# Output weights' preparation released earlier, and the first operand sums of a seven-product stage kept in other buffers

## The chip, the cores and the metric

One Trainium2 chip, one core of it. The metric is the device time of one execution in microseconds (us). The shown time before is the median of three runs.

## The reference

Sliding-window attention over 8 batches x 8 heads x 576 positions x 64 dimensions (window 128, a linear bias by distance and head), then a gated feed-forward layer over the 4608 tokens (512 in, 1536 hidden, 512 out), all in float32:

```python
x = attention(q, k, v).transpose(0, 2, 1, 3).reshape(4608, 512)
gate = 1.0 / (1.0 + exp(-(x @ w_gate)))
val = x @ w_val
return (gate * val) @ w_out
```

## The kernel before, in words

**Four kinds of work.** (1) Attention, 32 units (a batch and a pair of heads each). Its result goes to DRAM as `xs`, one piece per batch. (2) The *plain pass* (`ffn`, L646): for the first 3072 tokens, in six tiles of 512, four of the twelve hidden chunks are computed in the ordinary way. Each float32 operand is split into a high and a low part, and three matmuls (high*high, high*low, low*high) stand for one. (3) The *seven-product stage* (`ffn2` with `chunk` and `product`, L780): gate and value are computed together by a seven-product (Strassen-Winograd) scheme on 2x2 blocks. A token group (`GROUPS`: three of 2 x 512 tokens, then two of 2 x 384) is loaded from `xs` into `later_xr`, and eleven preparations follow: four block sums (`add`, L743) and seven splits into `xc0` to `xc6` (`hilo`, `parts`, L201 and L210), used in the order 0, 3, 4, 1, 5, 2, 6. Then each hidden chunk takes seven products of six matmuls, 42 in all, into three PSUM banks (`bx`, `by`, `bz`), with sums and gating on DVE and ACT (L787, L791, L795, and L201 for copies out of PSUM). The hidden rows go to DRAM (`hid`). The order of groups: the two of 384 first (groups 3 and 4, seven chunks each, then five more each), then the three of 512 (eight chunks each). (4) The *output stage* (`last`, L910) multiplies `hid` by the output weights, by the same scheme.

**Weights.** `prepare2` loads a chunk of gate and value weights (`wraw`, decoded at L337, L338, L341), forms four differences (L209 on POOL or L210 on DVE) and splits all seven blocks into a slot `w2s0` to `w2s6`. Slots 0 to 2 lie in a pool that is there from the start; slots 3 to 6 are in a pool that opens when the attention pool closes (`close`, key `"w2pool"`). `prepare_o(n)` does the same for the output weights, in six sets: load two raw chunks, decode into `wbits` and `tt`, four differences, split into `wg` and `wtmp`, store to DRAM as `stash_o`; `fetch_o(n)` later brings a set into slot n. Set n may not start before `OUT0 + OSTEP * n` on the planner's clock (470 + 36 n), and it has the lowest priority of all.

**What sets the order.** The kernel first builds a graph of operations with keys that they read and write, and a list scheduler (`Graph.order`) with a cost for each operation then fixes one order for every engine and for the DMA queue on SP. On the chip each engine, and SP, works through its list in that order. At equal start the operation with the lower `want` goes first: the plain pass has -1.0e6, the first seven-product group -1.0e6 + 0.4, later weights 0.5 to 0.9 above that, attention 0 to some 200, matmuls of the two stages 1.0e6, and `prepare_o` 2.0e6. A `follow(keys)` is an empty operation that writes all its keys: who uses one of them afterwards waits for all earlier users of any.

**Shared places.** `xc0` to `xc6` lie in the buffers `ar0` to `ar6`. Before that, the plain pass keeps its split tokens in `ar0` and `ar1` and its weights in `ar2` to `ar5` (one chunk each, used in the order 2, 3, 4, 5), and attention has the k and q of every third unit in `ar6`. `later_xr` has the buffer `xr`, in which the plain pass loads its tokens and attention has pieces too (`qr2`, `kept`, `spread2`, `xt0`). The scratch for sums, `low`, lies in `h2` with attention's `kr2`. The follow before `ffn2` makes both `xr` and `low` wait for `"w2pool"`. `wtmp0` and `wtmp1`, the large part of a `prepare_o` set, lie in `h3` and `h4`. In the last group of 512 (`ends`), a chunk's hidden rows rotate through four buffers `later_hs0` to `later_hs3` and not two; numbers 2 and 3 lie in `h3` and `h4` as well, so the third and fourth chunk of that group wait for the last set's stores out of `wtmp`.

**Banks.** Attention has PSUM banks 2 to 5 for scores and 6 and 7 for the rest; the plain pass has 0 and 1. The later stages take the eight in turn: 0, 1, 2, ... (`bank`).

Of the kernel before, what the change touches and what calls it, by code (L numbers as in the profile page):

```python
# [8 lines left out]
F32 = mybir.dt.float32  # L9
I32 = mybir.dt.int32  # L10
F32R = mybir.dt.float32r
# [4 lines left out]
P = 128  # L16
B, H, S, D = 8, 8, 576, 64
NPAIR = H // 2
TOK = 2 * S
NBLK = TOK // P  # L20
DM, DFF = 512, 1536
NT = B * S
KC = DM // P
NFC = DFF // P
NB = 512
# [14 lines left out]
KEEP2 = 3  # L40
NPB, NST, NPT, NBOTH = 8, 9, 3, 2
P0, PSTEP = 120.0, 56.0
OUT0, OSTEP = 470.0, 36.0
TRI = 3
VDELAY = 1
VHEAD = 11
# [124 lines left out]
def dve_cost(n, psum=False, two=False):  # L171
    return 0.07 + n * (0.00104 if psum or two else 0.00053)
# [7 lines left out]
def attention_gated_ffn(ctx: ExitStack, tc: tile.TileContext, qd, kd, vd, wg, wv, wo, out):  # L180
    nc = tc.nc
    ctx.enter_context(tc.manual_schedule())
    g = Graph()
# [3 lines left out]
    moe = ctx.enter_context(tc.tile_pool(name="moe", bufs=1))  # L187
    ps_m = ctx.enter_context(tc.tile_pool(name="ps_m", bufs=1, space=PSUM))
    att_ctx = ExitStack()
    att = att_ctx.enter_context(tc.tile_pool(name="att", bufs=1))  # L190
# [3 lines left out]
    def T(pool, name, shape, dtype, tag=None):  # L194
        if name not in made:
            made[name] = pool.tile(shape, dtype, tag=tag or name, name=name)
        return made[name]
# [35 lines left out]
    def keep(tag, *shape):  # L233
        n, (t, a) = 1, spare.get(tag) or (moe.tile([P, ROOM[tag]], F32, tag=tag, name=f"early_{tag}"), 0)
        for x in shape:
            n *= x
        spare[tag] = t, a + n
        names = " ".join("abc"[:len(shape)])
        return t[:, a:a + n].rearrange(f"p ({names}) -> p {names}", **dict(zip("abc", shape)))
# [4 lines left out]
    f = -8.0 * 2.0 ** -1  # L244
# [52 lines left out]
    class First:  # L297
        name, fcs = "w1", list(range(FC1))
# [7 lines left out]
    class Later:  # L306
        name = "w2"
# [6 lines left out]
    def piece_keys(a):  # L314
        keys = [(x, c) for x in ("xhi", "xlo") for c in range(KC)]
        keys += [("w1", kind, p, i) for i in range(FC1) for kind in "gv" for p in range(2)]
        return keys[a * PIECE:(a + 1) * PIECE]

    raws, mms, banks = [0], [0], [2]

    def bank():
        mms[0] += 1
        return (mms[0] - 1) % banks[0]

# [17 lines left out]
    def parts(hi, lo, val, n, reads, k0, k1, want, slack=0.0):  # L344
        copy(hi, val, n, reads, [k0], want, slack=slack)
        minus(lo, val, lambda: as32(hi()), n, [*reads, k0], [k1], want)
# [13 lines left out]
    class Unit:  # L360
# [12 lines left out]
        def rel(self, i):  # L373
# [4 lines left out]

    slots = {("kr", 2): keep("h2", TOK), ("qr", 2): keep("xr", (NBLK + 1) // 2, P),
             ("kr", 0): keep("ar6", TOK), ("qr", 0): keep("ar6", (NBLK + 1) // 2, P)}  # L380
    kept = [keep("h2", TRI, P), keep("xr", TRI, P)]
    spread2 = [keep("xr", TRI, P), keep("h2", TRI, P)]
    xt0 = keep("xr", S)

    def slot(x, u, shape):
        return slots[x, u.l] if (x, u.l) in slots else T(att, f"{x}{u.l}", [P, *shape], F32)
# [222 lines left out]
    FIRST = -1.0e6  # L609
# [66 lines left out]


    def combo(k, part_, n2):
        return T(moe, f"xc{k}", [P, 2, 2, NB], F32R, tag=f"ar{k}")[:, part_, :, 0:n2]

    def prepare2(w, i, fc, want, release=0.0):
        s = bitn[0] % 2
# [44 lines left out]
    def ffn2(t, w, todo, F, ends=False):  # L727
        made = t in held
        held[:] = [t]
        t0, N2 = GROUPS[t]  # L730
        xr = lambda: xrow()
# [4 lines left out]
        m = 2 * N2  # L736
# [3 lines left out]

        def add(o, a, b, op, reads, writes):
            way = ("POOL", 0.1 + m * 0.00223, True, lambda: nc.gpsimd.tensor_tensor(o(), a(), b(), op=op))
            g.add("DVE", dve_cost(m, two=True), lambda: nc.vector.tensor_tensor(o(), a(), b(), op=op), reads + ["w2pool"], writes, F,  # L743
                  port=True, ways=[way])

        if not made:
            for h in range(2):
                a = t0 + h * N2
                while a < t0 + (h + 1) * N2:
                    b = a // S  # L750
                    e = min((b + 1) * S, t0 + (h + 1) * N2)
# [3 lines left out]
                    a = e  # L755
# [78 lines left out]
    RAW = {(0, 0, 0): 0, (0, 0, 1): 1, (0, 0, 2): 2, (1, 0, 0): 3, (1, 1, 0): 7, (1, 0, 1): 8, (1, 1, 1): 11, (1, 0, 2): 9,  # L834
           (1, 1, 2): 10, (0, 1, 0): 4, (0, 1, 1): 5, (0, 1, 2): 6}

    HOMES = ((4, "xr", "xr", KC), (7, "w2s6", "w2s6", 3), (8, "hs0", "hs0", 1), (9, "hs1", "hs1", 1), (11, "ar6", "ar6", 2), (12, "h3", "h3", 1))

    def raw2(h, c, q, n2):
        z = RAW[h, c, q]  # L840
        for end, name, tag, n in HOMES:
            if z < end:
                return T(pools["w2"] if name == "w2s6" else moe, f"rows_{name}", [P, n, 2, NB], F32, tag=tag)[:, z - end + n, :, 0:n2]

    def csum(q, n2):
        return T(moe, f"csum{q}", [P, 2, NB], F32, tag=("wraw0", "wraw1", "tt")[q])[:, :, 0:n2]
# [3 lines left out]
    def last(t):  # L850
        F = FIRST + 2
        t0, N2 = GROUPS[t]
        n = 2 * N2
        for q in range(NDUO):
            for h, c in ((0, 0), (1, 0), (1, 1), (0, 1)):
                reads = [k for m in range(2) for k in g.writer if k[0] == "hid" and k[1] == 4 * q + 2 * m + c and k[2] == t]
# [6 lines left out]
        def add(o, a, b, op, reads, writes):  # L863
            way = ("POOL", 0.1 + n * 0.00223, True, lambda: nc.gpsimd.tensor_tensor(o(), a(), b(), op=op))
            g.add("DVE", dve_cost(n, two=True), lambda: nc.vector.tensor_tensor(o(), a(), b(), op=op), reads, writes, F, port=True, ways=[way])
# [17 lines left out]
        for k in ORDER:  # L883
            ring = []
            for q in range(NDUO):
                s, ks = (lambda q=q: csum(q, N2)), ("csum", q)
                k00, k01, k10, k11 = kx[0, 0, q], kx[0, 1, q], kx[1, 0, q], kx[1, 1, q]
                x00, x01, x10, x11 = x[0, 0, q], x[0, 1, q], x[1, 0, q], x[1, 1, q]
                if k == 3:
                    add(s, x10, x11, ALU.add, [k10, k11], [ks])  # L890
                elif k == 4:
                    add(s, s, x00, ALU.subtract, [k00], [ks])
                elif k == 5:
                    add(x10, x00, x10, ALU.subtract, [k00], [k10])
                elif k == 2:
                    add(x01, x01, s, ALU.subtract, [ks], [k01])
                val, key = {0: (x00, k00), 3: (s, ks), 4: (s, ks), 1: (x01, k01), 5: (x10, k10), 2: (x01, k01), 6: (x11, k11)}[k]
                r = RING[ducks[0] % len(RING)]
                ducks[0] += 1
                duo = lambda p, r=r: T(moe, f"duo{r}", [P, 2, 2, NB], F32R, tag=f"ar{r}")[:, p, :, 0:N2]  # L900
                parts(lambda duo=duo: duo(0), lambda duo=duo: duo(1), val, n, [key], ("ar", r, 0), ("ar", r, 1), F)
                ring.append((r, duo))
            for j in range(2):
                bx, by, bz = bks[j]
                b = {0: bx, 3: bz, 4: bx, 1: by, 5: bx, 2: bz, 6: bx}[k]
                for q, (r, duo) in enumerate(ring):
                    def six(q=q, duo=duo, b=b, j=j, k=k):
                        for m in range(2):
                            for e, (xp, wp) in enumerate(((0, 0), (0, 1), (1, 0))):
                                nc.tensor.matmul(mm[b][:, 0:N2], wo2(2 * q + m, wp)[:, k, j * P:(j + 1) * P], duo(xp)[:, m],  # L910
                                                 start=(k in (0, 3, 1) and q == 0 and m == 0 and e == 0),
                                                 stop=(q == NDUO - 1 and m == 1 and e == 2), skip_group_check=True)
                    g.add("PE", 6 * (N2 / 2400 + 0.0133), six, [("ar", r, 0), ("ar", r, 1)] +
                          [("w2", 2 * q + m, p, a) for m in range(2) for p in range(2) for a in (0, 2)],
                          [("mm", b), *(["seam"] if t == 0 and k == 0 else [])], 1.0e6)
                z = 4 * j
                if k == 0:
                    half(small(2 * j), bx, [("csmall", 2 * j)])
                elif k == 3:
                    half(ob(z), bz, [("cout", z)])  # L920
                elif k == 4:
                    half(small(2 * j + 1), bx, [("csmall", 2 * j + 1)])
                elif k == 1:
                    total(ob(z + 1), by, small(2 * j), [("csmall", 2 * j)], [("cout", z + 1)])
                    store(z + 1, 0, j, 0)
                elif k == 5:
                    total(ob(z), bx, ob(z), [], [("cout", z)])
                    store(z, 1, j, 1)
                elif k == 2:
                    total(ob(z + 2), bz, small(2 * j + 1), [("csmall", 2 * j + 1)], [("cout", z + 2)])  # L930
                    store(z + 2, 1, j, 0)
                else:
                    half(ob(z + 3), bx, [("cout", z + 3)])
                    store(z + 3, 0, j, 1)
# [35 lines left out]
        split_values(u, u.when(NBLK + 1), [], [], 0.0)()  # L970
    first_pass()

    pools = {}

    def close():
# [11 lines left out]
        prepare2(w2, i, stay[i], 2.0e6 + i, P0 + PSTEP * i)  # L987
    stash(0, stay[0])

    def follow(keys):  # L990
        g.add("PY", 0.0, lambda: None, [], keys, FIRST)

    for a in range(6):
        follow(piece_keys(a) + [("ar", a, j) for j in range(2)])
    follow(["w2pool", "s2", "a1", "u2", ("wtmp", 0), ("wtmp", 1), ("ar", 6, 0), ("ar", 6, 1)])
    later_xr = [("xr", k, (h, e)) for k in range(2) for h in range(2) for e in range(2)]
    follow([("xr", c, e) for c in range(KC) for e in range(2)] + ["w2pool"] + later_xr)
    for i in range(FC1):
        prepare2(w2, KEEP2 + i, first[i], FIRST + 0.5)
    if banks[0] == 2:  # L1000
        banks[0] = 8
        g.add("PY", 0.0, lambda: None, [], [("mm", z) for z in WORK], FIRST)
    head = list(zip(range(KEEP2), stay))
    body = list(zip(range(KEEP2, NSLOT2), first))
# [90 lines left out]
```

## Time and profile before

| | |
|---|---|
| median of 3 runs | 987.62 us (987.4 to 988.33) |
| the profiled execution, its own time | 988.12 us |
| its span, first to last instruction | 986.4 us |
| mean granted TensorE clock | 0.994 of full speed |
| TensorE (PE) busy | 962.8 us, 98% of the span |
| VectorE (DVE) busy | 793.7 us, 80% |
| ScalarE (ACT) busy | 509.4 us, 52% |
| GpSimd (POOL) busy | 126.8 us, 13% |

How to read it: times in a trace count from the span's first instruction. An engine's busy time is an average over stages with different limits, so it is read by stage below. "SPq" is the queue from which SP issues transfers. In a timeline, a bracket at a line's end gives the engine's idle time just ahead of the line and what ended it. The chain of work that ended last is followed back from the last instruction, and 64% of the span in it is PE.

### The profile page before, as it was taken

To read this page: it belongs to the slowest core of one execution; us is meant where nothing else is said; L and a number is where in the kernel's file an instruction comes from. 1 tells how busy PE (TensorE), PEld (TensorE's weight loads), DVE (VectorE), ACT (ScalarE), POOL (GpSimd) and SP (SyncE) were. 2 spreads that over 40 slices of the span, in tenths; PEclk is the share of its full clock that TensorE was granted. 3 is DMA by queue.
4 is the path that set the end of the run, shared out by engine and by line. 5 is a ranking of instruction groups with operands and counts; after the bars stand their busy time and mean duration, and the time that the engine had idled before them with its cause. 6 is when DMAs were issued, how large, how long until landed. Compare 5 with 4: busy or idle time off the path is not lost.

```text
span 986.4 us, 18539 instructions
## 1 busy us (share of the span) xinstructions
PE 962.8 (98%) x6592; PEld 835.3 (85%) x6592; DVE 793.7 (80%) x2014; ACT 509.4 (52%) x1324; POOL 126.8 (13%) x221
## 2 busy tenths in 40 slices
PE   8999999999999999999999999995999999999998
PEld 7677888888879999999988888884888888889998
DVE  8999989898978998867866867755498977877783
ACT  8999877878745454334533533522344433333341
POOL 3434343343320000000020000000000000000000
PEclk9999999999999999999999999997999999999999
DMA  8778768877645444233382373393986435162601
GB/s 299 259 235 305 234 214 293 276 230 243 206 135 177 141 141 135 98 139 134 131 302 118 124 292 150 107 355 119 393 294 194 157 109 192 60 197 80 193 17 64
DMA packets 82077, 186.03 MB, mean 189 GB/s; under 512 B 7744, under 2 KB 36800, under 8 KB 81984
## 3 DMA queue, kind: packets, MB, share of 16 engines
q1 hardware_dynamic: 81840, 184.71, 54.2%
q8 instruction: 52, 0.85, 0.4%
q14 instruction: 41, 0.34, 0.1%
q10 hardware_dynamic: 144, 0.13, 0.0%
HBM read 122.95 MB, written 61.87 MB: 187 GB/s over the span
## 4 chain that ended last, share of the span: by engine, by line
PE 64%; DVE 2%; DMA 1%; issue 0%; ACT 0%; ACTq 0%
PE mm L780 38%; PE mm L910 26%; DMA hid<-later_hs 0%; DVE wbits L341 0%; DVE mm L787 0%; DMA stash_o<-wtmp 0%; DVE w2s L210 0%; DMA stash_o<-wg 0%; DVE later_hs L795 0%; DVE later_hs L787 0%; ACT low L201 0%; DVE wbits L338 0%; DVE wtmp L202 0%; DVE low L743 0%; DVE later_xr L743 0%
## 5 line engine op out<-in xcount | busy, mean ns | idle before, releaser
L780 PE MATMUL mm<-xc,w2s 128*128 128x384 f32 (+1 forms) x2016 | 408.1, 364 | 12.2 <-ACT later_hs L201 9.2
L780 PEld LDWEIGHTS mm<-xc,w2s 128*128 128x128 f32 x2016 | 365.5, 189 | 54.6 <-ACT later_hs L201 9.7
L910 PE MATMUL mm<-duo,wo 128*128 128x512 f32 (+1 forms) x1260 | 258.9, 367 | 0.0
L910 PEld LDWEIGHTS mm<-duo,wo 128*128 128x128 f32 x1260 | 229.3, 188 | 29.5
L646 PE MATMUL mm<-first,first 128*128 128x512 f32 x576 | 154.0, 406 | 1.7 <-DVE first L210 1.3
L646 PEld LDWEIGHTS mm<-first,first 128*128 128x128 f32 x576 | 102.0, 188 | 25.2 <-DVE first L210 2.9
L787 DVE TENSOR_TENSOR mm<-mm,low 128x384 f32<-128x384 f32 (+1 forms) x96 | 60.1, 628 | 66.0 <-PE mm L780 65.4
L791 ACT ACTIVATE sg<-mm 128x384 f32<-128x384 f32 (+1 forms) x96 | 52.2, 545 | 114.9 <-PE mm L780 65.1
L201 ACT COPY low<-mm 128x384 f32<-128x384 f32 (+1 forms) x94 | 50.2, 534 | 82.5 <-PE mm L780 70.8
L475 ACT ACTIVATE pb<-pb,st 128x128 f32<-128x128 f32 x216 | 84.5, 396 | 5.4 <-DVE st L471 5.1
L571 POOL TENSOR_SCALAR_AFFINE_SELECT pt<-early_h 128x384 f32<-128x384 f32 x96 | 51.7, 558 | 112.6 <-ACT early_h L201 102.3
L571 POOL TENSOR_SCALAR_AFFINE_SELECT pt<-early_xr 128x384 f32<-128x384 f32 x96 | 51.9, 563 | 52.0 <-ACT early_xr L201 48.3
L463 DVE COPY_PREDICATED mm<-early_h,mm 128x256 f32<-128x256 int32 (+1 forms) x144 | 50.1, 389 | 4.0 <-PE mm L446 3.8
L471 DVE CUSTOM_DVE_ANT_0 pb<-mm,early_h 128x128 f32<-128x128 f32 x216 | 51.0, 280 | 0.0
L517 PEld LDWEIGHTS mm<-pt,vr 64*64 64x64 f32 x924 | 37.5, 133 | 9.1 <-issue 3.5
L795 DVE SCALAR_TENSOR_TENSOR later_hs<-sg,later_hs 128x384 f32<-128x384 f32 (+1 forms) x48 | 31.5, 656 | 15.7 <-ACT sg L791 15.7
L201 ACT COPY later_hs<-mm 128x512 f32<-128x512 f32 (+1 forms) x45 | 24.1, 535 | 36.9 <-PE mm L780 20.8
L475 ACT ACTIVATION_READ_ACCUMULATOR pb<-pb,st 128x1 f32 x216 | 41.5, 192 | 0.0
L517 PE MATMUL mm<-pt,vr 64*64 64x192 f32 (+2 forms) x924 | 41.4, 285 | 0.0
L201 ACT COPY early_xr<-mm 128x384 f32<-128x384 f32 (+3 forms) x76 | 32.9, 446 | 14.0 <-PE mm L517 9.8
L787 DVE TENSOR_TENSOR later_hs<-mm,later_hs 128x384 f32<-128x384 f32 (+1 forms) x48 | 29.8, 620 | 11.6 <-ACT sg L791 5.3
L553 DVE TENSOR_SCALAR pb<-pb,st 128x128 f32<-128x128 f32 x162 | 38.2, 286 | 0.2
(138 smaller groups left out, 1222.3 us busy)
## 6 DMA issues: line engine op xcount, KB each, us to landing
hid<-later_hs SPq DMA_DIRECT2D x24, 512.0 KB, 4.6
wo<-stash_o SPq DMA_DIRECT2D x12, 896.0 KB, 7.7
vr<-in_v_dram SPq DMA_DIRECT2D x32, 288.0 KB, 4.8
hid<-later_hs SPq DMA_DIRECT2D x24, 384.0 KB, 2.8
stash_o<-wtmp SPq DMA_DIRECT2D x12, 768.0 KB, 4.1
wraw<-in_moe_w_gate_dram SPq DMA_DIRECT2D x16, 512.0 KB, 4.6
wraw<-in_moe_w_val_dram SPq DMA_DIRECT2D x16, 512.0 KB, 4.2
kr<-in_k_dram SPq DMA_DIRECT2D x11, 576.0 KB, 4.7
```

The lines of the kernel that those rows point to most:

```text
L201: g.add("ACT", act_cost(n, psum), lambda: nc.scalar.copy(out(), src()), reads, writes, want, release=release, slack=slack, ways=[("DVE", d ...
L463: g.add("DVE", dve_cost((a1 - a0) * P, psum=True), lambda b=b, a0=a0, a1=a1: nc.vector.copy_predicated(quads(b)[:, a0:a1, 1:3], before[:, ...
L471: g.add("DVE", 0.21, lambda: nc.vector.tensor_tensor_reduce(pb()[:, e], sp[b][:, a, D:D + P], relm[u.p][:, w], op0=ALU.add, op1=ALU.min, s ...
L475: g.add("ACT", 0.39, lambda: nc.scalar.activation(pb()[:, e], pb()[:, e], AF.Exp, bias=st()[:, e:e + 1], scale=-1.0, accum_out=st()[:, 3 + ...
L517: nc.tensor.matmul(mm[WORK[h]][e * D:(e + 1) * D, a - e * S - cuts[h]:b - e * S - cuts[h]], vraw(u)[r * D:r * D + D, c], seen, start=first ...
L553: g.add("DVE", 0.19, lambda args=args: nc.vector.tensor_scalar_mul(*args()), [(kst, 6)], [(kpb, e)], want, port=True, ways=[("ACT", 0.3, F ...
L571: nc.gpsimd.affine_select(pt(u)[:, f0:f0 + 2 * n - 1:2, :], both(), [[0, n], step], cmp, 0.0, base=0, channel_multiplier=mult)
L646: nc.tensor.matmul(mm[s][:, 0:wd], w.tile(kind, wi, i)[:, c * P:(c + 1) * P], xpart(x, c)[:, 0:wd], start=(k == 0 and c == 0), stop=(k == ...
L780: nc.tensor.matmul(mm[b][:, 0:N2], w.tile2(i, wp)[:, wk, c * P:(c + 1) * P], combo(k, xp, N2)[:, c], start=(start and c == 0 and j == 0), ...
L787: g.add("DVE", dve_cost(N2, psum=True), lambda: nc.vector.tensor_tensor(o(), bk(b)(), a(), op=ALU.add), [("mm", b), *reads] if okeys else ...
L791: g.add("ACT", act_cost(N2, psum=True), lambda: nc.scalar.activation(sg[h](), bk(b)(), AF.Tanh, scale=0.5), [("mm", b)], [("sg", h)], F)
L910: nc.tensor.matmul(mm[b][:, 0:N2], wo2(2 * q + m, wp)[:, k, j * P:(j + 1) * P], duo(xp)[:, m], start=(k in (0, 3, 1) and q == 0 and m == 0 ...
```

## The change

It sets `OUT0` to 430. The sums `xc0` to `xc6` move to the buffers that `HOME` names: `xc0` to `ar6`, `xc3` to `ar2`, `xc4` to `ar3`, `xc1` to `ar4`, `xc5` to `ar5`, `xc2` to `ar0`, `xc6` to `ar1`; the output stage's `duo` and one of its row buffers follow. Attention's `kept1` and `spread0` go from `xr` into attention's own pool, and `xt0` into `h4`. The sums no longer read `"w2pool"`. The follows are set ahead of the closing of attention's pool, and each joins only the earlier and later users of one place. The banks of the later stages are taken in the order `ORD`, which begins with the score banks.

```diff
-OUT0, OSTEP = 470.0, 36.0
+OUT0, OSTEP = 430.0, 36.0
+HOME = (6, 4, 0, 2, 3, 5, 1)
+ORD = (2, 3, 4, 5, 0, 1, 6, 7)
...
         mms[0] += 1
-        return (mms[0] - 1) % banks[0]
+        return (mms[0] - 1) % 2 if banks[0] == 2 else ORD[(mms[0] - 1) % 8]
...
-    kept = [keep("h2", TRI, P), keep("xr", TRI, P)]
-    spread2 = [keep("xr", TRI, P), keep("h2", TRI, P)]
-    xt0 = keep("xr", S)
+    kept = [keep("h2", TRI, P), att.tile([P, TRI, P], F32, name="kept1")]
+    spread2 = [att.tile([P, TRI, P], F32, name="spread0"), keep("h2", TRI, P)]
+    xt0 = keep("h4", S)
...
-        return T(moe, f"xc{k}", [P, 2, 2, NB], F32R, tag=f"ar{k}")[:, part_, :, 0:n2]
+        return T(moe, f"xc{k}", [P, 2, 2, NB], F32R, tag=f"ar{HOME[k]}")[:, part_, :, 0:n2]
...
-            g.add("DVE", dve_cost(m, two=True), lambda: nc.vector.tensor_tensor(o(), a(), b(), op=op), reads + ["w2pool"], writes, F,
+            g.add("DVE", dve_cost(m, two=True), lambda: nc.vector.tensor_tensor(o(), a(), b(), op=op), reads, writes, F,
...
+    later_xr = [("xr", k, (h, e)) for k in range(2) for h in range(2) for e in range(2)]
+    follow([("xr", c, e) for c in range(KC) for e in range(2)] + [("qr", 2, i) for i in range(NBLK + 1)] + later_xr)
+    follow([("kr", 0, i) for i in range(NBLK)] + [("qr", 0, i) for i in range(NBLK + 1)] + [("ar", 0, j) for j in range(2)])
+    follow([("kr", 2, i) for i in range(NBLK)] + [(("pb", 0), e) for e in range(TRI)] + [("both", 1), "s2", "a1", "u2"])
+    for k in range(1, 7):
+        follow(piece_keys(HOME[k]) + [("ar", k, j) for j in range(2)])
...
-    for a in range(6):
-        follow(piece_keys(a) + [("ar", a, j) for j in range(2)])
-    follow(["w2pool", "s2", "a1", "u2", ("wtmp", 0), ("wtmp", 1), ("ar", 6, 0), ("ar", 6, 1)])
-    later_xr = [("xr", k, (h, e)) for k in range(2) for h in range(2) for e in range(2)]
-    follow([("xr", c, e) for c in range(KC) for e in range(2)] + ["w2pool"] + later_xr)
+    follow(["w2pool", ("wtmp", 0), ("wtmp", 1)])
...
-        banks[0] = 8
+        banks[0], mms[0] = 8, 0
```

## Rows read from the trace of the kernel before

**Rows 1.** The page's part 1: busy time of each engine over the span.
```profile
PE 962.8 (98%) x6592; PEld 835.3 (85%) x6592; DVE 793.7 (80%) x2014; ACT 509.4 (52%) x1324; POOL 126.8 (13%) x221
```

**Rows 2.** Busy us by stretch: PE, PEld, DVE, ACT, POOL, then clock, DMA.
```profile
283.00:304.00 21.00, 21.00 (x145) 16.81 (x144) 12.53 (x23) 6.01 (x11) 0.00 (x0) 1.00 0.48 163
304.00:326.00 22.00, 21.62 (x125) 21.30 (x124) 21.88 (x34) 12.38 (x23) 2.18 (x2) 1.00 0.52 168
...
367.00:384.00 17.00, 15.42 (x88) 14.78 (x86) 15.60 (x27) 8.92 (x18) 2.64 (x2) 1.00 0.55 177
...
430.00:480.00 50.00, 50.00 (x291) 50.00 (x290) 32.67 (x51) 21.72 (x40) 0.00 (x0) 1.00 0.35 123
...
480.00:500.00 20.00, 20.00 (x92) 16.90 (x92) 19.97 (x27) 11.27 (x19) 4.76 (x4) 1.00 0.64 226
```

**Rows 3.** The chain that ended last, in order of time: start, us, what.
```profile
384.19 287.37 PE mm L780 x1398
...
679.13 3.25 DMA stash_o<-wtmp
...
682.47 0.59 ACT later_hs L201
...
683.11 41.01 PE mm L780 x168
724.12 258.76 PE mm L910 x1260
```

**Rows 4.** Timeline of PE, 255 to 420 us: start, us, line, operation, count.
```profile
303.87 15.80 PE L780 MATMUL mm<-xc,w2s 128*128 128x384 f32 x90
320.05 54.79 PE L780 MATMUL mm<-xc,w2s 128*128 128x384 f32 x312 [0.38 <-DVE later_hs L787]
376.09 7.58 PE L780 MATMUL mm<-xc,w2s 128*128 128x384 f32 x42 [1.25 <-DVE later_hs L787]
```

**Rows 5.** Timeline of PE in the last group of 512, around its stop.
```profile
635.79 35.75 PE L780 MATMUL mm<-xc,w2s 128*128 128x512 f32 x157
...
672.21 1.66 PE L780 MATMUL mm<-xc,w2s 128*128 128x512 f32 x6 [0.68 <-ACT low L201]
```

**Rows 6.** Busy us in steps of 4 us at that stop, columns as in rows 2.
```profile
672.00:676.00 4.00, 1.66 (x6) 1.05 (x6) 3.14 (x7) 1.69 (x4) 0.00 (x0) 1.00 0.01 4
676.00:680.00 4.00, 0.00 (x0) 0.00 (x0) 3.90 (x8) 0.00 (x0) 0.00 (x0) 0.82 0.21 72
680.00:684.00 4.00, 0.89 (x2) 0.80 (x3) 1.58 (x2) 0.58 (x1) 0.00 (x0) 0.50 0.94 382
684.00:688.00 4.00, 4.00 (x11) 3.08 (x11) 1.39 (x2) 1.17 (x2) 0.00 (x0) 0.50 0.00 0
```

**Rows 7.** Raw output weights' loads (all twelve), then SP's queue around the fifth set.
```profile
L206 SPq DMA_DIRECT2D wraw<-in_moe_w_out_dram x12: 424/470/784, 476.7 to 659.0; - x12
...
617.60 0.42 SPq L206 DMA_DIRECT2D wraw<-in_moe_w_out_dram  x1
627.12 0.42 SPq L206 DMA_DIRECT2D wraw<-in_moe_w_out_dram  x1
...
651.40 2.59 SPq L206 DMA_DIRECT2D stash_o<-wtmp  x2
```

**Rows 8.** Timeline where the plain pass hands over its token buffer.
```profile
278.31 1.48 DVE L210 TENSOR_TENSOR first<-early_xr,first 128x512 fp32r<-128x512 f32 x2
...
291.65 0.98 SPq L206 DMA_DIRECT2D later_xr<-xs  x2
...
298.97 0.96 DVE L743 TENSOR_TENSOR low<-later_xr 128x768 f32<-128x768 f32 x1 [2.49 <-DMA later_xr<-xs]
```

**Rows 9.** Timeline of POOL and DVE ahead of the PE gap at 376 us.
```profile
369.62 1.86 POOL L742 TENSOR_TENSOR low<-later_xr 128x768 f32<-128x768 f32 x1 [37.95 <-ACT sg L791]
369.80 2.22 DVE L341 SCALAR_TENSOR_TENSOR wbits<-wraw,wbits 128x512 int32<-128x512 int32 x1
...
372.42 0.68 DVE L341 SCALAR_TENSOR_TENSOR wbits<-wraw,wbits 128x512 int32<-128x512 int32 x1
```

More of the change, by code (lines that the diff above doesn't have):

```diff
@@ L835, in attention_gated_ffn @@
            (1, 1, 2): 10, (0, 1, 0): 4, (0, 1, 1): 5, (0, 1, 2): 6}
-    HOMES = ((4, "xr", "xr", KC), (7, "w2s6", "w2s6", 3), (8, "hs0", "hs0", 1), (9, "hs1", "hs1", 1), (11, "ar6", "ar6", 2), (12, "h3", "h3", 1))
+    HOMES = ((4, "xr", "xr", KC), (7, "w2s6", "w2s6", 3), (8, "hs0", "hs0", 1), (9, "hs1", "hs1", 1), (11, "ar6", f"ar{HOME[6]}", 2), (12, "h3", "h3", 1))
     def raw2(h, c, q, n2):
@@ L899, in last @@
                 ducks[0] += 1
-                duo = lambda p, r=r: T(moe, f"duo{r}", [P, 2, 2, NB], F32R, tag=f"ar{r}")[:, p, :, 0:N2]
+                duo = lambda p, r=r: T(moe, f"duo{r}", [P, 2, 2, NB], F32R, tag=f"ar{HOME[r]}")[:, p, :, 0:N2]
                 parts(lambda duo=duo: duo(0), lambda duo=duo: duo(1), val, n, [key], ("ar", r, 0), ("ar", r, 1), F)
@@ L971, in attention_gated_ffn, with follow @@
     first_pass()
+    def follow(keys):
+        g.add("PY", 0.0, lambda: None, [], keys, FIRST)
+    later_xr = [("xr", k, (h, e)) for k in range(2) for h in range(2) for e in range(2)]
[4 more added lines that the diff above has]
+        follow(piece_keys(HOME[k]) + [("ar", k, j) for j in range(2)])
     pools = {}
@@ L988, in attention_gated_ffn @@
     stash(0, stay[0])
-    def follow(keys):
-        g.add("PY", 0.0, lambda: None, [], keys, FIRST)
-    for a in range(6):
-        follow(piece_keys(a) + [("ar", a, j) for j in range(2)])
-    follow(["w2pool", "s2", "a1", "u2", ("wtmp", 0), ("wtmp", 1), ("ar", 6, 0), ("ar", 6, 1)])
-    later_xr = [("xr", k, (h, e)) for k in range(2) for h in range(2) for e in range(2)]
-    follow([("xr", c, e) for c in range(KC) for e in range(2)] + ["w2pool"] + later_xr)
+    follow(["w2pool", ("wtmp", 0), ("wtmp", 1)])
     for i in range(FC1):
```

## The prediction, made before the changed kernel ran

> **What bounds the kernel now.** I read the page's busy shares first: PE is busy for 98% of the span [rows 1]. A share that high says little by itself, so I next asked where in the span the other 2% lies, and what PE does elsewhere. The chain of waits, in order of time, answers both [rows 3]. From 384.19 us to the end it is PE almost alone: 1398 matmuls without a break for 287.37 us, then a hole, then 168 matmuls, then the 1260 of the output stage in 258.76 us. The reader is to see that only two places are left in which anything but matmul throughput sets the end: the hole, and the stretch before 384.
>
> The hole first. PE stops after the six matmuls of 672.21 and starts again at 683.11; the chain shows why: a store out of `wtmp` (3.25 us), then the ACT copy into `later_hs` for which it made room, then PE [rows 3, 5]. This is the sixth `prepare_o` set. Its work is what DVE does in that hole, 3.14 + 3.90 + 1.58 us, with hardly anything else [rows 6]. When PE comes back its granted clock is 0.50, the lower level of 1.2 GHz, through 688 us [rows 6].
>
> The stretch before 384 is the two groups of 384. Here DVE is the crowded engine: 21.88 of 22 us and 15.60 of 17 [rows 2], and PE's gaps end on DVE's L787 [rows 4]. In the stretch just before, 283 to 304, DVE is busy for only 12.53 of 21 us and ACT for 6.01 [rows 2], while PE is full with the plain pass. That idle DVE time is what the second half of the change can use. PE goes from the plain pass (L646) straight into the seven products at 303.87 [rows 4], so nothing can be won at the handover itself.
>
> **The change part by part.**
>
> *OUT0 from 470 to 430.* Nothing is added or removed; six sets move by 40 us. Are sets tied to their release? The first raw load is at 476.7, the last at 659.0 [rows 7], five steps of 36 apart by the program, 182 us by the trace: yes, some 7 to 9 us behind the planner's clock. So the sixth set, released at 610, falls 4 us ahead of where the fifth stood (released at 614). The fifth loaded at 617.60 and 627.12 and its `wtmp` stores were issued from 651.40 [rows 7]; with a landing like the 3.25 us of rows 3, the sixth set's buffers are free by about 656, against 682.4 now.
>
> Who needs them? The last group starts at 635.79, and 157 matmuls take 35.75 us [rows 5], 0.2277 us each and 9.56 us a chunk. The third chunk starts at 654.9, and its first copy into `later_hs` is due two products (12 matmuls, 2.7 us) later, at 657.6; 2 us sooner if the earlier stage gains what I give it below. So the buffer comes about when it is wanted. It may be a few us late, but now PE had other chunks' products to run until 671.6 [rows 3], 14 us past that point, so a small lateness is covered. If the plan kept no such products at hand, a lateness of 3 us would cost 3 us.
>
> The price of the hole: from the end of the 1398 (384.19 + 287.37 = 671.56) to 724.12 are 52.56 us, for 6 + 168 = 174 matmuls. At 0.2277 they need 39.6. So 12.9 us are lost: 0.68 + 9.2 us idle (672.21 + 1.66 to 683.11), and 41.01 - 168 x 0.2277 = 2.8 us in the 168 for the lower clock. Bounds of the gain: 0 (the last set still last) to 12.9. I take 12.9, because the fifth set's rows lie 4 us behind the new sixth and they fit.
>
> What the moved sets meet: set n lands near the old n - 1. The old first, 480 to 500, lay beside the sums of a 512 group, with DVE at 19.97 of 20 and PE at 20.00 [rows 2]: such company cost nothing. Only the new first set meets something new, the 384 stage from about 437 us. There DVE is busy for 32.67 of 50 us [rows 2]; a set is 8.6 us of DVE [rows 6], so 41.3 of 50. Bounds: nothing, or what the same stage lost when DVE was full, 0.38 us in 22 and 1.58 in 17 [rows 2]. I take 0.3 us, near the smaller: 83% is not 99%. Its two loads and four stores on SP find DMA at 0.35 there [rows 2]. SP issues in order, so a store of hidden rows queued behind a `wtmp` store waits for DVE with it; the old sets had the same neighbours at no cost to PE. In the last group the `fetch_o` transfers no longer stand behind the sixth set's stores, so they start sooner; nobody waited for them in the chain [rows 3].
>
> *Sums ahead of the closing.* Now the tokens of the first group are loaded at 291.65 and used at 298.97, 7.3 us later; the token buffer was free from 278.31 + 1.48 = 279.8 [rows 8]. So the load can go up to 11.8 us sooner and the sums from about 287. By place, `xc0`, `xc3` and `xc4` and the sums they need, and one more sum, can be done before 304: six DVE instructions of 0.96 us [rows 8], 5.8 us, into 21.00 - 12.53 = 8.5 us of idle time [rows 2]. DVE then enters the crowded stretch 5.8 us ahead. PE's 90 + 312 + 42 = 444 matmuls from 303.87 to 384.19 [rows 3, 4] take 80.3 us; at 50.00/291 = 0.172 us [rows 2] they need 76.3, so 4.0 us are lost there, and PE can get no more back. Bounds: 4.0 gained, or up to 2 lost where the new order puts a DVE sum of 0.96 us ahead of what PE waits for, twice. I take 2.0 gained, half: 5.8 us of lead outweighs the 4.0 lost, but the four later slots' weights still queue on the same DVE, and the gap at 376 has a cause that the lead does not touch (rivals).
>
> *Edits with one answer:* the bank order only renames banks at an equal distance of reuse, and the moved attention tiles take no other engine time: 0, covered by PE's unbroken run up to 303.87 [rows 4].
>
> Sum: -12.9 - 2.0 + 0.3 = -14.6 us. Against the profiled execution's own 988.12: 973.5. That execution lies 0.5 us above the median of the runs, 987.62, so the median should be 973.0 us.
>
> **A rule weighed against the trace.** At 369.62 POOL has one of the sums for 1.86 us; the DVE instruction that starts beside it takes 2.22 us, where the same one takes 0.68 at 372.42 [rows 9]. It stands ahead of the 1.25 us PE gap at 376.09 [rows 4]. The Trainium skill, "SBUF — State Buffer", section "Who interferes with whom", says that a DVE instruction with two SBUF inputs and a GpSimd instruction reading SBUF shut each other out until the first is done. By that rule the trace agrees, and a set moved into the 384 stage costs it DVE time twice over. By the rows of DVE's load alone that term is the 0.3 us above; by the rule it is nearer the 5 us of the third rival.
>
> **The rivals.**
>
> *The sixth set is still late* (chance 0.12). Its release is only a lower bound: the fifth set took 34 us from first load to last store [rows 7], squeezed by the next group's sums. If the sixth is held until 665 to 670, PE gets some of its idle time back, without the clock's part if the stop is short: 3 to 6 us, 976 to 979. Against: the 14 us of other products.
>
> *No help at the seam* (0.10). The order there is rewritten, and DVE stays full for as long as slots 3 to 6 are unprepared. Gain 0, or a loss up to 2: 975 to 977.
>
> *POOL against DVE in the 384 stage* (0.04). The old first set ran beside 4.76 us of POOL in four instructions [rows 2]. If each stretches a DVE instruction by 2.22 - 0.68 = 1.5 us, 6 us of DVE are added near 440; with the set's 8.6 and two thirds of the time taken already, most would fall on PE's waits: 5 us, 978.
>
> *Slower: PE's order at the seam* (0.05). PE's list is fixed. With score banks and `ar6` free early, the plan may put first products among the plain pass's last tile. Place: 280 to 304. If their tokens come no earlier than now (the load behind attention's stores, 291.65), operands exist at about 301 [rows 8], and PE may stand from as early as 280 with the plain pass's matmuls behind the waiting one: up to 21 us, plus the 2.8 of a fallen clock, 24 in all: 997. It turns the sign once wait plus clock exceed 14.6, a stop of some 12 us. For it: PE never skips a waiting matmul. Against: up to now PE met its plan here without a gap [rows 4].
>
> **How the numbers follow.** The forecast, both terms much as priced, has 0.69. Its low end is 988.12 - 12.9 - 4.0 - 0.5 = 970.7. The range 970.5 to 977.5 takes in the forecast's own bounds, the second rival and the near half of the first. About 0.2% (2.0 us) is what a measurement of this kernel can tell from no change: faster is below 985.6, slower above 989.6. Faster 0.92; the same 0.03, from the far end of the sixth set staying last and the slow rival's small stops; slower 0.05.
>
> **What would show it.** Raw loads of output weights from about 437 to 620 and the last `wtmp` stores issued by about 655; the chain with no `stash_o` in it, and PE unbroken from about 384 to 982 at full granted clock; token loads by 285; PE's gaps between 304 and 384 adding up to 2 us in place of 4. The prediction is wrong if a stop of more than 3 us stays near 660 to 680, if PE waits anywhere in 280 to 304, or if gaps appear near 440.

## The result, and the profile after

The changed kernel takes 974.17 us (median of 4 runs, 971.1 to 976.04) against 987.98 (4 runs, 987.4 to 990.28): a ratio of 0.9853, 95% interval 0.9822 to 0.9883. The forecast was 973.0, between 970.5 and 977.5. The profiled execution took 974.72 us, 13.4 less than the one before.

The page's part 1, which answers to [rows 1]:
```profile
PE 959.7 (99%) x6592; PEld 833.3 (86%) x6592; DVE 791.0 (81%) x2016; ACT 510.4 (52%) x1326; POOL 123.0 (13%) x217
```

The chain that ended last, in order of time (start, us, what), answering to [rows 3]:
```profile
304.82 393.85 PE mm L782 x1974
701.62 8.76 DMA hid<-later_hs
710.39 6.39 DMA rows_h<-hid
716.88 1.24 DVE csum L867
...
721.69 247.76 PE mm L912 x1210
```
PE's timeline from the plain pass's last piece on:
```profile
289.55 15.27 PE L648 MATMUL mm<-first,first 128*128 128x512 f32 x66
304.65 403.68 PE L782 MATMUL mm<-xc,w2s 128*128 128x384 f32 x2016
708.17 11.80 PE L912 MATMUL mm<-duo,wo 128*128 128x512 f32 x50
```
The seven-product stage is now one piece: all its 2016 matmuls run without a break, and 1974 of them stand in the chain. The store out of `wtmp` is gone from the chain. New is what stands at the start of the output stage: a store of hidden rows that takes 8.76 us, the load of those rows that waits for it, a sum of them on DVE, and only then PE.

Busy us by stretch, columns as in [rows 2]:
```profile
283.00:304.00 21.00, 21.00 (x160) 16.82 (x153) 16.04 (x28) 9.42 (x16) 0.23 (x1) 1.00 0.49 174
304.00:326.00 22.00, 22.00 (x128) 21.88 (x126) 21.28 (x38) 11.12 (x20) 0.00 (x0) 1.00 0.54 175
367.00:384.00 17.00, 17.00 (x100) 16.97 (x99) 16.27 (x29) 7.63 (x15) 0.00 (x0) 1.00 0.43 144
430.00:480.00 50.00, 50.00 (x290) 49.91 (x289) 40.19 (x64) 24.13 (x45) 0.74 (x1) 1.00 0.50 176
...
650.00:690.00 40.00, 40.00 (x178) 33.14 (x177) 16.66 (x25) 11.85 (x20) 0.00 (x0) 1.00 0.87 312
...
720.00:724.00 4.00, 2.31 (x10) 1.94 (x11) 4.00 (x5) 2.00 (x2) 0.00 (x0) 1.00 0.84 328
```
PE is full in the two groups of 384 and where the hole was, 650 to 690. DVE is still crowded from 304 on (21.28 of 22), but PE no longer waits for it. The 1.69 us missing at 720 are the new stop.

SP's queue in the timeline, answering to [rows 7, 8]:
```profile
280.62 0.92 SPq L208 DMA_DIRECT2D later_xr<-xs  x2
...
437.69 1.17 SPq L208 DMA_DIRECT2D wraw<-in_moe_w_out_dram  x2
...
614.79 1.25 SPq L208 DMA_DIRECT2D wraw<-in_moe_w_out_dram  x2
...
648.60 2.58 SPq L208 DMA_DIRECT2D stash_o<-wtmp  x2
...
700.67 0.89 SPq L208 DMA_DIRECT2D wo<-stash_o  x2
701.62 0.42 SPq L208 DMA_DIRECT2D hid<-later_hs  x1
...
710.39 0.37 SPq L208 DMA_DIRECT2D rows_h<-hid  x1
```
The first group's tokens are asked for 11 us sooner than before, the sets of output weights run from 437.69 to 614.79, and the last `wtmp` stores are issued at 648.60. The last lines show the new wait: the hidden rows' store is issued right behind two fetches of 896 KB, and the row load cannot go before it has landed.

### The profile page after: what moved, and what is told of

Its sections match the earlier page's. It is cut to its first block, busy times and chain, and to the rows that moved or that the text cites. A ratio compares the mean times of both kernels' runs of the same rounds, so it can differ in the third digit from the quotient of the medians.

```text
span 973.0 us, 18554 instructions
## 1 busy us (share of the span) xinstructions
PE 959.7 (99%) x6592; PEld 833.3 (86%) x6592; DVE 791.0 (81%) x2016; ACT 510.4 (52%) x1326; POOL 123.0 (13%) x217
## 4 chain that ended last, share of the span: by engine, by line
PE 90%; DVE 7%; DMA 2%; issue 0%; ACT 0%; SPq 0%; DVEq 0%; ACTq 0%
PE mm L782 40%; PE mm L912 25%; PE mm L648 13%; PE mm L448 4%; PE mm L519 3%; PE mm L562 3%; PE mm L600 1%; DVE pb L473 1%; DVE mm L465 1%; DMA hid<-later_hs 1%; DVE pb L555 1%; DMA rows_h<-hid 1%; DVE first L212 1%; DVE wbits L343 0%; DMA early_ar<-in_q_dram 0%; DVE st L550 0%
## 5 line engine op out<-in xcount | busy, mean ns | idle before, releaser
L782 PE MATMUL mm<-xc,w2s 128*128 128x384 f32 (+1 forms) x2016 | 403.7, 362 | 0.0
L203 ACT COPY low<-mm 128x512 f32<-128x512 f32 (+1 forms) x94 | 50.3, 535 | 64.5 <-PE mm L782 63.3
L573 POOL TENSOR_SCALAR_AFFINE_SELECT pt<-spread 128x384 f32<-128x384 f32 x96 | 51.8, 562 | 51.7 <-ACT spread L203 51.2
L203 ACT COPY early_h<-mm 128x384 f32<-128x384 f32 (+3 forms) x75 | 32.2, 444 | 15.6 <-PE mm L519 9.9
L211 POOL TENSOR_TENSOR tt<-tt 128x256 f32<-128x256 f32 x9 | 9.9, 1099 | 216.7 <-DVE tt L212 216.5
```

The lines of the kernel that those rows point to most:

```text
L203: g.add("ACT", act_cost(n, psum), lambda: nc.scalar.copy(out(), src()), reads, writes, want, release=release, slack=slack, ways=[("DVE", d ...
L573: nc.gpsimd.affine_select(pt(u)[:, f0:f0 + 2 * n - 1:2, :], both(), [[0, n], step], cmp, 0.0, base=0, channel_multiplier=mult)
L782: nc.tensor.matmul(mm[b][:, 0:N2], w.tile2(i, wp)[:, wk, c * P:(c + 1) * P], combo(k, xp, N2)[:, c], start=(start and c == 0 and j == 0), ...
```

## The experiments

The theory to test: three separate places. The hole closes through `OUT0`; the gaps from 304 to 384 close through the lead of the sums; the new stop comes with the earlier sets. All times are medians; the kernel before was measured beside each group (989.43 us for the first four, 988.44 for the others).

**1. `OUT0` alone.** In the kernel before:
```diff
-OUT0, OSTEP = 470.0, 36.0
+OUT0, OSTEP = 430.0, 36.0
```


> The kernel before with OUT0 at 430 and nothing else. My theory (three separate places): the hole of 12.9 us in the last group of 512 closes, the two groups of 384 still lose about 4 us between 304 and 384, and the new wait of some 2.6 us at the start of the output stage is there, because it comes with the earlier last set: 988 - 12.9 + 2.6 = 977 to 978. Rival (the edits only work together: without the lead at the seam the last set is late again): the hole stays in part and the time is 980 or more. Rival (the new wait comes from the bank order or the moved sums): no wait there, 975.

Measured: 977.25 us, ratio 0.988 (0.9852 to 0.9907). PE's timeline:
```profile
320.76 6.79 PE L780 MATMUL mm<-xc,w2s 128*128 128x384 f32 x36 [0.37 <-DVE later_hs L787]
328.01 48.14 PE L780 MATMUL mm<-xc,w2s 128*128 128x384 f32 x276 [0.46 <-DVE later_hs L787]
377.57 7.56 PE L780 MATMUL mm<-xc,w2s 128*128 128x384 f32 x42 [1.42 <-DVE later_hs L787]
385.88 327.10 PE L780 MATMUL mm<-xc,w2s 128*128 128x384 f32 x1572 [0.75 <-ACT low L201]
...
726.82 3.47 PE L910 MATMUL mm<-duo,wo 128*128 128x512 f32 x14 [1.72 <-DVE duo L210]
```
The gaps of [rows 4] are all still there, the hole is not (the 1572 matmuls run through its place), and the output stage has the new stop of 1.72 us. So the hole and the stop both belong to `OUT0`, without the sums or the banks.

**2. The sums alone.** In the changed kernel:
```diff
-OUT0, OSTEP = 430.0, 36.0
+OUT0, OSTEP = 470.0, 36.0
```


> The changed kernel with OUT0 back at 470. My theory: PE runs without a gap from 304 to 384 (4 us gained), the hole before the last sets' stores stays at about 13 us, no wait at the start of the output stage: 988 - 4 = 984. Rival (nothing is gained at the seam unless the sets move too): 987 to 988. Rival (the whole gain is in the seam's rewritten order, which also moves the hole): under 980.

Measured: 985.99 us, ratio 0.9972 (0.9957 to 0.9986). PE's timeline, then the top of the list of waits (engine, line, what it waited for: us in total, times, longest):
```profile
304.28 121.04 PE L782 MATMUL mm<-xc,w2s 128*128 128x384 f32 x697
...
720.89 259.21 PE L912 MATMUL mm<-duo,wo 128*128 128x512 f32 x1260
```
```profile
PE mm L782 <- ACT later_hs L203: 9.3, 1, 9.3
```
The other half of the same picture: no gap from 304 on, the hole of 9.3 us back, no stop at the output stage. The gain is 3.4 us. The ratios of experiments 1 and 2 multiply to 0.9852, and the whole change has 0.9853: within the noise the two parts add up, as separate places should.

**3. The sums in the new places, but not early.**
```diff
-            g.add("DVE", dve_cost(m, two=True), lambda: nc.vector.tensor_tensor(o(), a(), b(), op=op), reads, writes, F,
+            g.add("DVE", dve_cost(m, two=True), lambda: nc.vector.tensor_tensor(o(), a(), b(), op=op), reads + ["w2pool"], writes, F,
...
-    follow(["w2pool", ("wtmp", 0), ("wtmp", 1)])
+    follow(["w2pool", ("wtmp", 0), ("wtmp", 1), "s2", "a1", "u2"] + later_xr)
```


> The changed kernel, but the first group's token load and its sums wait for the closing of attention's pool again, as before; places, banks and OUT0 as changed. If the lead of the sums is what filled the gaps between 304 and 384, they come back: 2 to 4 us idle on PE there, and the time is 976 to 978. If the other places or the bank order did it, PE stays unbroken there and the time is that of the changed kernel, 971 to 976.

Measured: 979.23 us, ratio 0.9897 (0.9873 to 0.9921), a little over the expected 978. PE's timeline:
```profile
304.85 62.16 PE L782 MATMUL mm<-xc,w2s 128*128 128x384 f32 x356
367.64 15.77 PE L782 MATMUL mm<-xc,w2s 128*128 128x384 f32 x88 [0.63 <-DVE xc L212]
384.60 40.68 PE L782 MATMUL mm<-xc,w2s 128*128 128x384 f32 x233 [1.19 <-ACT low L203]
```
Gaps return. The 356 + 88 = 444 matmuls that took 80.3 us before take 384.60 - 304.85 = 79.75 here. At experiment 2's unbroken rate, 121.04 / 697 = 0.1737 us, they need 77.1: of 3.2 us lost before, 2.6 are back. It was the lead that filled the gaps, not the places. But it did so in two ways. Of the 2.6 us, 0.9 are lost before 367.64 and 1.7 after it, and there POOL again has one of the later block sums:
```profile
370.82 4.82 POOL L744 TENSOR_TENSOR low<-later_xr 128x768 f32<-128x768 f32 x1 [54.39 <-DMA later_xr<-xs]
```
In all three kernels without the lead and with this choice left open (before, experiments 1 and 3) the planner gives that sum to POOL; in the changed kernel (DVE, 371.45, 0.95 us) and in every experiment with the lead it does not. So part of the lead's gain came by way of the planner's choice, and this experiment alone doesn't separate the two; experiment 7 bears on it.

**4. Banks in plain order.**
```diff
-ORD = (2, 3, 4, 5, 0, 1, 6, 7)
+ORD = (0, 1, 2, 3, 4, 5, 6, 7)
```


> The changed kernel with the banks of the later stages in the order 0 to 7. My prediction priced the bank order at 0: time as the changed kernel's, 971 to 976, PE unbroken from 304 on. Rival (the score banks, free earlier, are what lets the first products run without a gap): gaps of 1 to 3 us between 300 and 330.

Measured: 975.71 us, ratio 0.9861 (0.9836 to 0.9887); PE is unbroken from 303.99 through all 2016 matmuls. The bank order is worth nothing that can be measured.

**5. The changed kernel again,** as the measure for the next three.

> The changed kernel as it is, on the chip of the next three, as their measure. 971 to 976 as before; a PE stop of 1.7 us at the start of the output stage again, since it is in the order of SP's queue and not in chance.

Measured: 975.31 us (973.01 to 978.52), and the stop of 1.71 us again; there another row load, of `rows_xr`, is the last to land behind the store. Its profiled execution took 978.52; the clock shows where the rest went (4 us steps, columns as in rows 2):
```profile
38.00:42.00 4.00, 3.82 (x25) 2.31 (x17) 4.00 (x16) 3.00 (x13) 0.31 (x2) 0.55 0.35 141
42.00:46.00 4.00, 4.00 (x43) 3.19 (x39) 2.72 (x12) 1.91 (x7) 0.91 (x2) 0.60 0.38 131
...
724.00:728.00 4.00, 4.00 (x11) 3.13 (x12) 4.00 (x4) 1.46 (x2) 0.00 (x0) 0.57 0.40 155
```
What follows is in the last section.

**6. The store ahead of the fetches.** In the changed kernel's graph alone:
```diff
-            gated(p5, p5, [], [kp], 1, False)
+            gated(p5, p5, [], [kp, ("sent", t, fc)], 1, False)
...
-                 [("stash_o", n, p, e) for e in range(2)], [("w2", n, p, 0), ("w2", n, p, 2)], FIRST + 1.5, 896, True)
+                 [("stash_o", n, p, e) for e in range(2)] + [("sent", SPLIT - 1, SLOTFC[n])], [("w2", n, p, 0), ("w2", n, p, 2)], FIRST + 1.5, 896, True)
...
+    SLOTFC = dict(head[1:] + [(0, here)] + body)
     for n in range(NFC // 2):
```


> The changed kernel, but in the planner's graph each fetch of output weights in the last group also waits for the gating that makes the chunk's hidden rows ready, so that SP issues the store of hidden rows ahead of the two fetches of 896 KB and not behind them. My theory (the stop of PE at the output stage is the store's 8.8 us behind the fetches, then the row load that waits for it): the store lands in 3 to 5 us, PE's stop at the output stage is under 0.5 us, time 2 to 3 us under the changed kernel's. Rival (the order of the sums on DVE makes the stop, whatever the store does): the stop stays at 1.7 us, same time. Rival (the fetches, now later, become what the output stage waits for): a stop of 1 to 4 us on the output weights.

Measured: 972.01 us (971.87 to 975.07), ratio 0.9845 (0.9826 to 0.9863). SP's queue, then the chain:
```profile
699.64 0.32 SPq L208 DMA_DIRECT2D hid<-later_hs  x1
700.05 1.22 SPq L208 DMA_DIRECT2D wo<-stash_o  x2
702.61 0.37 SPq L208 DMA_DIRECT2D rows_h<-hid  x1
```
```profile
707.88 258.76 PE mm L912 x1260
```
The store lands within 3.0 us (the row load that waits for it goes at 702.61), where it took 8.76. PE's stop is gone, and the output stage takes 258.76 us as in [rows 3]. No wait on the output weights took its place. Up to the sum that needs the late row DVE's list is that of the changed kernel, and DVE no longer idles ahead of it (6.2 us there, against a stop of 1.7), so the order of the sums alone does not make the stop. Behind that sum the list was planned anew. This version is faster than the kernel before. Against the changed kernel the trace shows the stop gone and the median beside it is 3.3 us lower, but the two ratios' intervals overlap.

**7. Block sums kept off POOL,** in the kernel before (`add` of `ffn2`):
```diff
-                  port=True, ways=[way])
+                  port=True, ways=[])
```


> The kernel before, with the block sums of the seven-product stage kept off POOL (one of them ran there, at 369.6 us). If POOL and DVE shut each other out, and this made the PE gap of 1.25 us at 376 us, no DVE instruction beside it is stretched to 2.2 us any more and that gap goes: 987 to 988, about 1 us less than before. Rival (DVE is late there anyway, the gap is DVE's load): a gap of 1 us or more stays between 365 and 385, same time.

Measured: 987.47 us, ratio 0.9997 (0.9984 to 1.0011). DVE in the timeline, then PE:
```profile
371.37 0.68 DVE L341 SCALAR_TENSOR_TENSOR wbits<-wraw,wbits 128x512 int32<-128x512 int32 x1
```
```profile
328.14 97.18 PE L780 MATMUL mm<-xc,w2s 128*128 128x384 f32 x558 [0.44 <-DVE later_hs L787]
```
The DVE instruction of 2.22 us [rows 9] takes 0.68, and the gaps of 1.25 and 0.52 us that PE had at 376 and 384 are gone: 558 matmuls in a row. Of the 3.2 us that the first 444 matmuls lost before, 1.5 stay (the first 126 take 328.14 - 304.73 = 23.4 us and need 21.9) and the rest is gone. The time saved, about 1 us of median, is inside the interval. The rest of the order was planned anew as well, so all of the second gap need not be POOL's.

**8. `OUT0` halfway,** at 450 in the changed kernel:
```diff
-OUT0, OSTEP = 430.0, 36.0
+OUT0, OSTEP = 450.0, 36.0
```


> The changed kernel with OUT0 halfway, at 450: the last set's stores are issued some 10 to 15 us later than with 430, about 660 to 665, after the third chunk of the last group wants its buffer. My theory (PE has other chunks' products for 14 us past that point): PE idles under 1 us between 650 and 690, time as the changed kernel's. Rival (PE stops as soon as the buffer is late): a stop of 5 us or more there, time over 978.

Measured: 975.94 us, ratio 0.9876 (0.9853 to 0.9899). SP's queue, ACT and PE in the timeline:
```profile
663.58 2.11 SPq L208 DMA_DIRECT2D stash_o<-wtmp  x2
```
```profile
655.72 0.59 ACT L203 COPY low<-mm 128x512 f32<-128x512 f32 x1 [0.70 <-PE mm L782]
...
668.44 0.59 ACT L203 COPY later_hs<-mm 128x512 f32<-128x512 f32 x1
```
```profile
599.76 111.83 PE L782 MATMUL mm<-xc,w2s 128*128 128x512 f32 x492
```
The last set's stores are issued 15 us later than with 430. The third chunk's copy into `later_hs` was due about 657.1, one product (1.4 us) behind its first copy at 655.72, and came at 668.44: 11 us late. PE does not stop: 492 matmuls in a row through the place. A buffer late by that much is covered by other chunks' products. The output stage's stop is shorter here, 0.88 us, and stands behind another row load.

## Why the prediction was right, point by point

| step | predicted | measured |
|---|---|---|
| hole in the last group | -12.9 | -12.9: no stop in it, matmuls at the full rate |
| sums ahead of the closing | -2.0 | -3.7: what the stage gained (420.25 to 403.68 us, 16.6) beyond the hole |
| first set in the 384 stage | +0.3 | 0: PE 50.00 of 50 |
| bank order, moved tiles | 0 | 0 (experiment 4, for the banks) |
| start of the output stage | 0 | +2.4 |
| attention | 0 | +0.8 |
| sum | -14.6 | -13.4, as between the profiled executions |

That the sum comes so near is in part luck: 1.7 us more from the sums and 0.3 less for the first set stand against 2.4 and 0.8 us that were put at nothing.

*The hole* went as worked out, and for the reason given: sets follow their release, and the last stores came at 648.60, inside "by about 655". They took 7.4 and 7.8 us to land, not the 3.25 assumed, so the buffers came free at about 656 all the same. The third chunk's copy was due about 653.8 and came at 657.21: a few us of the cover of 14 us, on which the forecast leaned, were used, and experiment 8 shows that 11 us of it hold. There the stores landed at about 668 and 670, within the 665 to 670 of the first rival (the set is still late), and PE lost nothing: its price of 3 to 6 us was too high.

*The sums* were mis-sized: half of the loss was taken, all of it came (3.7 us by the traces, 3.4 by experiment 2's medians). Two numbers of the working were off. At 0.1737 us a matmul the first 444 lost 3.2 us, not 4.0: the 291 counted in 50.00 us take in matmuls that the stretch cuts. And DVE's lead was not 5.8 us: sums and splits already ran from 298.97 in the kernel before, and DVE's busy time from 283 to 304 rose by 3.5 us, from 12.53 to 16.04. Experiments 2 and 3 show that the lead is the cause. I held half back because the gap at 376 seemed to have a cause that the lead does not touch. There was such a cause, by experiment 7 worth about half of the loss; what failed is the step that it would stay. The POOL instruction is a choice of the planner's, and with the sums early the planner did not make it.

*The first set in the 384 stage* cost nothing, although DVE went from 32.67 to 40.19 of 50 us, close to the 41.3 worked out. The third rival needed the old set's 4.76 us of POOL in that stretch; the planner gave POOL 0.74. In experiment 1 POOL had 2.29 us there, and PE was still busy for 50.00 of 50. The Trainium skill's "SBUF — State Buffer", section "Who interferes with whom", says that a DVE instruction with two SBUF inputs and a GpSimd instruction that reads SBUF contend. Experiment 7 agrees with it where POOL did run (2.22 us beside POOL, 0.68 without). That the 4.76 us would have cost PE anything is not shown.

*The slow rival* did not happen: PE goes from the plain pass into the seven products at 304.65 without a gap.

*What was missed:* "In the last group the `fetch_o` transfers no longer stand behind the sixth set's stores, so they start sooner; nobody waited for them". True of the fetches, but the question was who stands behind them. The store of hidden rows did, and the output stage's first sums wait for those rows. The store stood behind the fetches before as well; there DVE had another sum to do first, of `rows_ar`, and PE did not stop:
```profile
729.98 1.22 DVE L865 TENSOR_TENSOR csum<-rows_ar 128x1024 f32<-128x1024 f32 x1
731.36 1.23 DVE L865 TENSOR_TENSOR csum<-rows_hs,rows_h 128x1024 f32<-128x1024 f32 x1 [0.17 <-DMA rows_h<-hid]
```
Now DVE's list has the late rows first, and it idles 6.2 us for them:
```profile
716.88 1.23 DVE L867 TENSOR_TENSOR csum<-rows_hs,rows_h 128x1024 f32<-128x1024 f32 x1 [6.18 <-DMA rows_h<-hid]
```
So two things made the stop, the late rows and a list with nothing to do ahead of them. Experiment 1 puts the stop with `OUT0`; experiment 6 shows that the store's place in the queue suffices to remove it. It costs 2.4 us: 721.69 + 247.76 - 708.33 = 261.1 us for the output stage, against 258.76.

The other +0.8 is the start of the seven products, 304.65 against 303.87; executions of one kernel differ by more than that (last section). What made it is not shown.

## What to carry to other kernels

When a stop of the bound engine is traced to a late buffer, ask how far past its due time the order still gives that engine other work: here 11 us of lateness cost nothing. Work moved into an idle stretch in front of a crowded one can be worth all of the loss behind it; where a scheduler makes the order anew, a second cause that the change doesn't touch, here a sum on POOL, may go with it. And of every transfer that starts sooner, ask what is issued behind it on the same queue and who reads that: a store of 512 KB behind two fetches of 896 KB took 6 us longer to land, and issuing it ahead of them removed the stop.

## What the runs showed of the hardware that was not expected

The granted clock fell in attention's start, in some executions more than in others, though the program there issues the same operations. In the changed kernel's first profile, 4 us steps:
```profile
38.00:42.00 4.00, 3.53 (x24) 2.81 (x25) 4.00 (x19) 2.31 (x10) 1.02 (x2) 0.61 0.14 53
42.00:46.00 4.00, 4.00 (x44) 3.17 (x41) 3.52 (x19) 3.28 (x9) 0.87 (x2) 0.97 0.82 236
```
In its second profile (experiment 5) it was 0.55 and 0.60 in the same steps, and in the kernel before 1.00. PE had gaps just before in all three (busy for 2.54 or 2.55 of the 4 us from 34). The changed kernel's seven products then began at 304.65 and 306.87: 2.2 us between two executions of one program, which no edit made. The late starts go with a fall that lasts both steps, as in experiment 8 (0.54 and 0.60, start 306.76). A shorter fall does not show in the start: it was 303.99 in experiment 4 with 0.70 in the first step, and 304.85 in experiment 3 with 1.00 in both.

The stop of 1.71 us at the output stage was followed by a fall of the clock, 0.57 from 724 to 728, in the second profile and not in the first, though it was as long in both. Experiments 1, 3 and 4 had the stop too, and the clock was 1.00 in the steps behind it. The same short stop thus cost 2.4 us in one execution and about 4 in the other (the last 1210 matmuls took 249.35 us and 247.76).
